# Bias-table reads moved behind four loads, the identity ahead on the SyncE queue, and new landing times in a hand-written plan (T5 attention, then a squared-ReLU FFN)

## The chip, the core and the metric

The kernel runs on one core of a Trainium2 chip. The metric is device time in microseconds (us), the median over several runs. A profile is one execution recorded by the hardware; its times are counted from the first instruction. Engines are named as in the profile: PE (TensorE matmuls), PEld (TensorE weight loads), DVE (VectorE), ACT (ScalarE), POOL (GpSimd, which here only issues DMAs), SP (SyncE, likewise).

## What is computed

Eight batches of attention with eight heads, 576 positions and head size 64, with a bias that depends on the distance of two positions, and then a feed-forward net on all 4608 rows:

```python
scores = scale * np.matmul(q, k.transpose(0, 1, 3, 2))
bias = bias_table[bucket]            # bucket of |i - j|; 31, the last, from 128 on
scores = scores + bias.transpose(2, 0, 1)[None]
attn = exp(scores - max) / (sum + 1e-09)
x = (attn @ v).transpose(0, 2, 1, 3).reshape(4608, 512)
out = np.maximum(x @ w_in, 0.0) ** 2 @ w_out      # 512 -> 2048 -> 512
```

## The kernel before

**Units.** Attention is cut into 96 units: a batch, a block of 192 queries and a pair of heads. A unit's scores are ten PE matmuls (`st`, lines 615 and 640); ACT takes their exponential in two pieces of 960 and 768 columns (`et`, line 666); DVE multiplies the band near the diagonal by exp(bias) from a table `tb_sb` (lines 684 and 698); ten matmuls multiply by V and give the sums as well (`pv`, line 774); ACT makes the reciprocal by a logarithm and an exponential (`r`, lines 816 and 846); DVE multiplies (`x_sb`, line 827). When a block of 192 rows has all four of its head pairs, layer 1 can start on it (`hps`, line 902: eight matmuls to a group, evicted and squared by ACT and DVE in lines 913 to 921), and later layer 2 (`yps`, line 985; eviction in line 998; output by SP in line 1001).

**Loads.** K and Q of the first two batches come in as pairs of heads by POOL's DMAs (`kh`, `qh`, line 251) and are transposed on PE against an identity `id_sb` (line 502; evictions in lines 517 and 519; small copies in line 554). The very first pair of K comes through SP as `raw` and is cast by DVE (line 392). V goes to `vz`, the weights to `w_in_sb` and `w_out_sb`, all by POOL's one queue, in the order in which `load_qk`, `load_v`, `table_read` and `load_w_in` are called (lines 376 to 459). Batches from the third on are transposed by SP's DMAs.

**The bias table.** `bt_sb` and `far_sb` arrive by ACT's queue; DVE subtracts (line 400), ACT exponentiates (line 403), one matmul against a one-hot matrix `oh_sb` spreads the 32 buckets over 512 distances (line 409), DVE casts (line 414), and SP writes the result to memory as `t_bias` (line 418). Three POOL DMAs then read it back as overlapping rows into `tb_sb` (line 421): heads 0 and 1, 2 and 3, and 4 to 7. The first of them waits for SP's write, and POOL issues in order, so what is behind it waits too.

**The order.** Every instruction is an `Op` with an engine, the time that it occupies it, its latency, what it depends on and when it is due. `Plan.run` (line 139) walks through all of them once, at build time, with those numbers, and writes the instructions of each engine in the order that it finds. On the chip each engine runs its list strictly in that order. So a number in the plan takes no time itself, but it sets what stands ahead of what. A load's landing is planned as `dma = max(dma, at + 1.35) + o.load; o.done = dma + 1.9` (lines 175 to 177); before, a pair of Q or K is planned at 1.2 us of the DMA engines, a V load at 1.02 us, and a table read at 0.3 us for each head. `plan.fill` (line 471) puts matmuls that compute nothing needed (`warm`, line 367) wherever PE would be idle in the plan before the first `pv`.

Of the kernel before, what the change touches and what calls it, by code (L numbers as in the profile page):

```python
# [30 lines left out]
PT, TPP = 96, 6  # L31
# [9 lines left out]
F1_LAG, F2_LAG = 4.8, 19.5  # L41

NEXT = 4.0
START = {"POOL": 1.25, "DVE": 0.85, "PE": 1.25, "ACT": 2.9, "SP": 0.3}

MODE = 0.095
WAIT = {"ACT": 0.15, "DVE": 0.05}
# [44 lines left out]
class Plan:  # L92
# [46 lines left out]
    def run(self):  # L139
        free = {**dict.fromkeys(self.streams, 0.0), **START}  # L140
        dma, rows, held = 0.0, 128, None
        while any(q for x in self.streams.values() for q in x.values()):
# [31 lines left out]
            free[eng] = at + o.occ  # L174
            if o.load:
                dma = max(dma, at + 1.35) + o.load
                o.done = dma + 1.9
            if o.instead:
                o.instead()
            self.order.append(o)  # L180
# [4 lines left out]
def kernel(  # L185
# [10 lines left out]
    nc = tc.nc  # L196
# [53 lines left out]
    def dma(eng, out_, in_):  # L250
        return lambda: io(eng.dma_start(out=out_, in_=in_))  # L251
# [4 lines left out]
    def load_qk(b, h0, n, which="kq"):  # L256

        return [
            pool(
                dst[:, h0 : h0 + n, :],  # L260
                src[b, h0 : h0 + n].rearrange("h (p t) d -> p h (t d)", t=TPP),
                0.6 * n,
            )
            for dst, src, name in zip(h16s[b][::-1], (k, q), "kq")
            if name in which
        ][::-1]

    def load_v(b, h, deps=()):

        vz = vzs[b % 2]  # L270
        e, o = h % 2, 64 * (h % 2)
        loads = [
            pool(
                vz[:, 0:4, h, o : o + 64],
                v[b, h, 0:512, :].rearrange("(t p) d -> p t d", p=128),
                1.02,
                deps,
            )
        ]
# [49 lines left out]
    for out_, in_, t in (  # L329
        (bt_sb, bias_table, 3.2),  # L330
        (far_sb, bias_table[NBK - 1 : NBK, :].to_broadcast([NBK, H]), 3.6),
    ):
        dma(nc.scalar, out_, in_)()
        small_in.append(Op("ACT", 0.0, 0.0, None, []))
        small_in[-1].at, small_in[-1].done = 0.0, t
# [22 lines left out]
            )  # L358
        ]

    def small(out_, in_, lat):
        return add("SP", "set", 0.5, lat, dma(nc.sync, out_, in_))
# [52 lines left out]


    loads_qk[0, 4] = loads_qk[0, 5] = load_qk(0, 4, 2)
    written = add("SP", "set", 0.45, 3.5, dma(nc.sync, tdram.ap(), tv_sb), [tv])
    loads_v[0] = [x for h in range(2) for x in load_v(0, h, vz_set[0])]

    def table_read(h0, n):
        return pool(
            tb_sb[:, h0 : h0 + n, :],
            bass.AP(tensor=tdram, offset=512 * h0 + 1, ap=[[1, 128], [512, n], [1, 384]]),
            0.3 * n,
            [written],
        )

    def table_mixed(e):

# [659 lines left out]
```

## Time and profile before

| What | us |
|---|---|
| median of 5 runs | 425.76 (424.82 to 428.29) |
| the profiled execution, as timed | 425.89 |
| its span, first to last instruction | 424.1 |
| PE busy in the span | 407.8 (96%) |
| DVE busy | 315.0 (74%) |
| ACT busy | 302.5 (71%) |
| POOL busy (issuing) | 130.7 (31%) |

The page cuts the span into 40 slices of 10.6 us and gives each engine's busy share in tenths. A window view gives the busy time of each engine in stretches that the reader chooses, with the TensorE clock that was granted there (PEclk, 1.00 is full speed). A timeline lists instructions in order of time, equal neighbours merged, with the idle time before them and what ended it. For a DMA the timeline shows the time in which it is issued; the landing is later, and the view of DMA issues gives the time from the one to the other.

### The profile page before, as it was taken

The page shows a single profiled execution, that of the slowest core. Times are in us where ns is not written, and L with a number is a line of the kernel's source. Part 1 is how long each engine was busy: PE and PEld are TensorE (multiplying, and loading weights), DVE is VectorE, ACT ScalarE, POOL GpSimd, SP SyncE. Part 2 cuts the span into 40 slices and gives each one's busy share as a digit, 9 for nine tenths or more (in the row PEclk, how much of TensorE's full clock was granted, in tenths as well). Part 3 has the DMA queues.
Part 4 walks back from the last instruction along what each step waited for, and adds up shares of the span by engine and source line. Part 5 has one row for each costly group of instructions (what it writes and reads, how often), then busy time and mean ns, then how long its engine had stood idle before and what let it go on. Part 6 is the DMA issues. An engine that isn't in the chain of part 4 may idle for free.

```text
span 424.1 us, 9453 instructions
## 1 busy us (share of the span) xinstructions
PE 407.8 (96%) x3631; PEld 261.9 (62%) x3631; DVE 315.0 (74%) x940; ACT 302.5 (71%) x588; POOL 130.7 (31%) x176
## 2 busy tenths in 40 slices
PE   7979999999899999999999999999999999999996
PEld 4656786566675666666666666665666666565554
DVE  6778866578775777787778787787787877778762
ACT  5899878786797888778877778768877878771000
POOL 6955829606800193006700193006000000000000
PEclk8899999999999999999999999999999999999999
DMA  9999999989982499068974599167203201001012
GB/s 124 157 199 141 152 146 87 111 87 138 125 91 67 73 119 122 28 105 101 105 74 67 104 87 127 38 103 89 38 29 73 64 9 42 22 6 51 25 51 74
DMA packets 164765, 36.61 MB, mean 86 GB/s; under 512 B 152584, under 2 KB 160064, under 8 KB 164720
## 3 DMA queue, kind: packets, MB, share of 16 engines
q0 software_dynamic: 129728, 19.11, 59.5%
q1 hardware_dynamic: 34896, 16.90, 17.3%
q8 instruction: 28, 0.46, 0.5%
q14 instruction: 17, 0.14, 0.1%
q10 hardware_dynamic: 96, 0.00, 0.0%
HBM read 37.56 MB, written 16.52 MB: 128 GB/s over the span
## 4 chain that ended last, share of the span: by engine, by line
PE 78%; DVE 8%; ACT 7%; DMA 4%; issue 2%; SPq 0%; POOLq 0%
PE yps L985 27%; PE hps L902 26%; PE pv L774 13%; PE st L640 6%; ACT et L666 4%; PE pv L748 3%; PE st L615 2%; DMA kt<-k 2%; DVE x_sb L827 2%; ACT r L816 2%; DVE et L684 2%; DMA tb_sb<-t_bias 1%; DVE rt L921 1%; DVE y L998 1%; DVE km_sb L554 1%
## 5 line engine op out<-in xcount | busy, mean ns | idle before, releaser
L666 ACT ACTIVATE et<-st 128x960 f16<-128x960 f32 x192 | 167.9, 882 | 58.9 <-PE st L640 58.1
L902 PE MATMUL hps<-x_sb,w_in_sb 128*128 128x384 f16 (+1 forms) x896 | 150.9, 303 | 1.4 <-DVE rt L921 0.9
L985 PE MATMUL yps<-w_out_sb,g_sb 128*128 128x512 f16 (+1 forms) x592 | 148.5, 373 | 1.8 <-DVE y L998 1.6
L902 PEld LDWEIGHTS <-w_in_sb 128*128 128x128 f16 x896 | 83.0, 98 | 50.8 <-issue 3.6
L684 DVE TENSOR_TENSOR et<-et,tb_sb 128x384 f16<-128x384 f16 (+2 forms) x288 | 78.3, 311 | 35.0 <-ACT et L666 30.4
L251 POOL DMA_DIRECT2D vz<-in_v_dram x80 | 57.9, 744 | 131.6 <-PE pv L774 72.2
L985 PEld LDWEIGHTS <-g_sb 128*128 128x128 f16 x592 | 57.1, 98 | 49.1 <-issue 4.0
L774 PE MATMUL pv<-et,vz 128*128 128x192 f16 x804 | 84.0, 247 | 1.7 <-DVE et L684 1.1
L827 DVE TENSOR_TENSOR x_sb<-pv,r 64x192 f16<-64x192 f32 x192 | 67.8, 353 | 23.2 <-ACT r L846 20.1
L917 DVE TENSOR_TENSOR g_sb<-rt 128x384 f16<-128x384 f16 x192 | 67.5, 355 | 7.9 <-ACT rt L913 4.1
L774 PEld LDWEIGHTS <-vz 128*128 128x128 f16 x804 | 62.0, 98 | 17.2 <-issue 14.6
L816 ACT ACTIVATE r<-pv 64x192 f32<-64x192 f32 x192 | 62.4, 325 | 8.4 <-PE pv L774 3.6
L913 ACT ACTIVATE rt<-hps 128x384 f16<-128x384 f32 x93 | 45.3, 487 | 26.0 <-PE hps L902 25.1
L921 DVE TENSOR_SCALAR rt<-hps 128x384 f16<-128x384 f32 x99 | 55.2, 557 | 11.0 <-PE hps L902 7.3
L640 PE MATMUL st<-qt,kt 64*128 64x192 f16 x768 | 51.0, 246 | 1.6 <-ACT et L666 1.6
L251 POOL DMA_DIRECT2D k<-in_k_dram x48 | 31.0, 682 | 26.0 <-DMA q<-in_q_dram 13.5
L846 ACT ACTIVATE r<-r 128x192 f32<-128x192 f32 x96 | 34.8, 363 | 3.0
L640 PEld LDWEIGHTS <-kt 64*128 64x128 f16 x768 | 31.9, 95 | 4.9 <-issue 3.2
L998 DVE TENSOR_SCALAR y<-yps 128x512 f32<-128x512 f32 (+1 forms) x37 | 25.0, 675 | 7.2 <-PE yps L985 6.5
L615 PEld LDWEIGHTS <-km_sb 128*128 128x128 f16 x192 | 18.3, 98 | 19.0 <-issue 3.8
L615 PE MATMUL st<-qt,km_sb 128*128 128x96 f16 x192 | 24.1, 208 | 1.8 <-ACT et L666 1.1
L251 POOL DMA_DIRECT2D q<-in_q_dram x18 | 24.6, 1401 | 0.0
(33 smaller groups left out, 118.9 us busy)
## 6 DMA issues: line engine op xcount, KB each, us to landing
out_dram<-y SPq DMA_DIRECT2D x35, 256.0 KB, 2.5
vz<-in_v_dram POOLq DMA_DIRECT2D x64, 64.0 KB, 3.4
q<-in_q_dram POOLq DMA_DIRECT2D x18, 192.0 KB, 8.1
k<-in_k_dram POOLq DMA_DIRECT2D x48, 72.0 KB, 7.1
w_in_sb<-in_moe_w_in_dram POOLq DMA_DIRECT2D x4, 512.0 KB, 10.0
w_out_sb<-in_moe_w_out_dram POOLq DMA_DIRECT2D x4, 512.0 KB, 10.0
qh<-in_q_dram POOLq DMA_DIRECT2D x8, 144.0 KB, 6.9
kh<-in_k_dram POOLq DMA_DIRECT2D x7, 144.0 KB, 7.6
```

Of the source, the lines that this page charges most:

```text
L251: return lambda: io(eng.dma_start(out=out_, in_=in_))
L615: nc.tensor.matmul(st[:, g, 2 * IC : 2 * IC + IC // 2], km_sb[:, p % KB, :], qts[p][:, ds(c0 + g * IC // 2, IC // 2)], start=True, stop=True,)
L640: nc.tensor.matmul(st[:, e, ds(i * IC, IC)], kts[p][rows, ts(2 * g + i, 128)], qts[p][rows, ds(c0, IC)], start=True, stop=True,)
L666: io(nc.scalar.activation(out=et, in_=sts[n, g][:, :, 0:w], func=EXPF, scale=SCALE))
L684: nc.vector.tensor_tensor(out=sl, in0=sl, in1=tb_sb[:, 2 * hp : 2 * hp + 2, ds(w0, w)], op=MULT)
L774: nc.tensor.matmul(pv if jt < 4 else pv.rearrange("p (g c) -> p g c", g=2), vz[:, jt, 2 * hp + e, :], ets[n, jt // 2][:, e, ds(jt % 2 * IC ...
L816: nc.scalar.activation(out=rs[n][o : o + 64, :], in_=pvt[n, e][64 - o : 128 - o, 0:IC], func=LNF)
L827: nc.vector.tensor_tensor(out=x_sb[o : o + 64, hp, ds(ring(blk), IC)][:, ::-1], in0=pvt[n, e][o : o + 64, 0:IC], in1=rs[n][o : o + 64, :], ...
L902: nc.tensor.matmul(hps[:, ds(i * w, w)], w_in_sb[:, kk, ts(nt, 128)], x_sb[:, kk, ds(o, w)], start=(kk == 0), stop=(kk == 3),)
L917: io(nc.vector.tensor_tensor(out=g_sb[:, ts(u, k), o : o + w], in0=rt, in1=rt, op=MULT))
L921: io(nc.vector.tensor_scalar_max(out=rt, in0=hpt[blks, u][:, 0 : 2 * IC], scalar1=0.0))
L985: nc.tensor.matmul(ypt[j], g_sb[:, nt, ds(128 * m % RING, 128)], w_out_sb[:, nt, cols], start=(nt == 0), stop=(nt == 15),)
```

## The change

Five edits; the arithmetic is the same.

1. On POOL's queue the V loads of heads 2 and 3 and the K and Q loads of heads 6 and 7 move ahead of the first two table reads, and the V loads of heads 4 and 5 ahead of the third.
2. On SP's queue the identity is issued first, ahead of `raw`.
3. The one-hot matrix `oh_sb` moves from SP's queue to ACT's, as the third DMA there, ahead of the load of ACT's function table.
4. Planned landing times: a Q or K load 0.46 us for each head where it was 0.6, a V load 0.6 and 0.3 where it was 1.02 and 0.5, a table read 0.5 for each head where it was 0.3, 2.0 us after the transfer where it was 1.9, the write of `t_bias` 2.6 us where it was 3.5, `raw` 3.3 where it was 3.4.
5. ACT is planned to be free from 3.3 us on, where it was 2.9.

```diff
-START = {"POOL": 1.25, "DVE": 0.85, "PE": 1.25, "ACT": 2.9, "SP": 0.3}
+START = {"POOL": 1.25, "DVE": 0.85, "PE": 1.25, "ACT": 3.3, "SP": 0.3}
-                o.done = dma + 1.9
+                o.done = dma + 2.0
-                0.6 * n,
+                0.46 * n,
-                1.02,
+                0.6,
-                    0.5,
+                    0.3,
         (far_sb, bias_table[NBK - 1 : NBK, :].to_broadcast([NBK, H]), 3.6),
+        (oh_sb, oh_d.ap(), 4.5),
+    id_in = add("SP", "set", 0.45, 2.8, dma(nc.sync, id_sb, id_d.ap()))
     k_raw = add(
-        "SP", "set", 0.45, 3.4, dma(nc.sync, raw, k[0, 0:2].rearrange("h (p t) d -> p h (t d)", t=TPP))
+        "SP", "set", 0.45, 3.3, dma(nc.sync, raw, k[0, 0:2].rearrange("h (p t) d -> p h (t d)", t=TPP))
     )
-    small_in.append(small(oh_sb, oh_d.ap(), 2.8))
-    id_in = small(id_sb, id_d.ap(), 2.8)
...
-    written = add("SP", "set", 0.45, 3.5, dma(nc.sync, tdram.ap(), tv_sb), [tv])
+    written = add("SP", "set", 0.45, 2.6, dma(nc.sync, tdram.ap(), tv_sb), [tv])
...
-            0.3 * n,
+        return pool(tb_sb[:, h0 : h0 + n, :], rows, 0.5 * n, [written])
...
+    loads_v[0] += [x for h in range(2, 4) for x in load_v(0, h)]
+    loads_qk[0, 6] = loads_qk[0, 7] = load_qk(0, 6, 2)
+    tbs = [table_read(0, 2), table_read(2, 2)]
+    loads_v[0] += [x for h in range(4, 6) for x in load_v(0, h)]
+    tbs += [table_read(4, 4)] * 2
+    loads_v[0] += [x for h in range(6, 8) for x in load_v(0, h)]
...
-    tbs = [table_read(0, 2), table_read(2, 2)]
-    loads_v[0] += [x for h in range(2, 4) for x in load_v(0, h)]
-    loads_qk[0, 6] = loads_qk[0, 7] = load_qk(0, 6, 2)
-    tbs += [table_read(4, 4)] * 2
-    loads_v[0] += [x for h in range(4, 8) for x in load_v(0, h)]
```

Edits 4 and 5 change numbers of the plan alone, and with them the written order on PE, ACT and DVE, all the way to the end of the kernel.

More of the change, by code (lines that the diff above doesn't have):

```diff
@@ L359, in ones @@
         ]
-    def small(out_, in_, lat):
-        return add("SP", "set", 0.5, lat, dma(nc.sync, out_, in_))
     warm = psP.tile([128, 512], FP32, tag="p1", name="warm")
@@ L417 @@
     loads_qk[0, 4] = loads_qk[0, 5] = load_qk(0, 4, 2)
-    written = add("SP", "set", 0.45, 3.5, dma(nc.sync, tdram.ap(), tv_sb), [tv])
+    written = add("SP", "set", 0.45, 2.6, dma(nc.sync, tdram.ap(), tv_sb), [tv])
     loads_v[0] = [x for h in range(2) for x in load_v(0, h, vz_set[0])]
     def table_read(h0, n):
-        return pool(
-            tb_sb[:, h0 : h0 + n, :],
-            bass.AP(tensor=tdram, offset=512 * h0 + 1, ap=[[1, 128], [512, n], [1, 384]]),
-            0.3 * n,
-            [written],
-        )
+        rows = bass.AP(tensor=tdram, offset=512 * h0 + 1, ap=[[1, 128], [512, n], [1, 384]])
+        return pool(tb_sb[:, h0 : h0 + n, :], rows, 0.5 * n, [written])
[5 more added lines that the diff above has]
+    loads_v[0] += [x for h in range(6, 8) for x in load_v(0, h)]
     def table_mixed(e):
```

## The prediction

> **What bounds the kernel now.** I read the page's busy shares first (PE 96%), then windows, to see which stage has room, then the timelines of POOL, DVE and ACT around the table reads, then the landings of the single DMAs. The windows; the columns are length, then busy time and instructions of PE, PEld, DVE, ACT and POOL, the granted PE clock, and the DMA share and rate:
>
> ```profile
> 4.58:8.00 3.42, 2.42 (x45) 1.73 (x47) 2.34 (x9) 2.00 (x6) 2.75 (x5) 1.00 1.25 166
> 8.00:11.41 3.41, 3.10 (x48) 1.99 (x48) 2.20 (x7) 3.26 (x5) 1.43 (x3) 0.50 0.86 61
> 11.41:14.82 3.41, 3.41 (x41) 2.15 (x39) 1.69 (x5) 2.47 (x4) 3.41 (x6) 0.50 1.15 162
> ...
> 15.00:25.00 10.00, 8.28 (x108) 6.41 (x107) 9.61 (x34) 8.66 (x20) 8.27 (x12) 1.00 1.34 183
> 25.00:42.74 17.74, 14.64 (x194) 10.74 (x194) 13.54 (x45) 17.26 (x35) 10.12 (x15) 1.00 1.26 163
> 42.74:60.00 17.26, 16.22 (x216) 14.24 (x215) 13.20 (x42) 13.32 (x29) 10.09 (x12) 1.00 1.42 156
> ...
> 200.00:420.00 220.00, 219.40 (x1765) 134.86 (x1764) 165.84 (x477) 144.99 (x283) 34.14 (x44) 1.00 0.47 61
> ```
>
> From 200 us on PE is busy 219.40 of 220.00: PE is the bound there, and a change can only move the end by letting PE do more useful work early. PE's idle time is in the start: 1.72 of 10.00 us, 3.10 of 17.74, 1.04 of 17.26. In those stages others are the bound: DVE at 9.61 of 10.00 from 15 to 25 us, ACT at 17.26 of 17.74 from 25 to 42.74. Before 15 us the first bias multiply holds everything, as these timelines show, one of POOL, then one of DVE, ACT and PE:
>
> ```profile
> 4.59 2.73 POOL L251 DMA_DIRECT2D vz<-in_v_dram  x4
> 9.98 1.45 POOL L251 DMA_DIRECT2D tb_sb<-t_bias  x2 [2.65 <-DMA t_bias<-tv_sb]
> 11.41 1.53 POOL L251 DMA_DIRECT2D vz<-in_v_dram  x2
> ...
> 17.87 0.83 POOL L251 DMA_DIRECT2D w_in_sb<-in_moe_w_in_dram  x1
> ```
>
> ```profile
> 15.00 2.72 DVE L684 TENSOR_TENSOR et<-et,tb_sb 128x384 f16<-128x384 f16 x12 [1.18 <-DMA tb_sb<-t_bias]
> ...
> 19.89 0.84 DVE L519 CAST kt<-tp 128x288 f16<-128x288 f32 x2
> ...
> 22.22 0.48 DVE L519 CAST qt<-tp 128x288 f16<-128x288 f32 x1
> 22.75 0.26 PE L615 MATMUL st<-qt,km_sb 128*128 128x96 f16 x2 [0.72 <-DVE qt L519]
> 23.33 0.97 ACT L666 ACTIVATE et<-st 128x960 f16<-128x960 f32 x1 [0.54 <-PE st L640]
> 29.19 0.83 PE L902 MATMUL hps<-x_sb,w_in_sb 128*128 128x192 f16 x8
> ```
>
> POOL stands for 2.65 us until SP's write of the table has landed, and all loads behind it are late by as much: V of heads 2 and 3, K and Q of heads 6 and 7, the weights. The fourth head pair is then transposed and evicted in the stage where DVE is the bound (19.89, 22.22), and ACT starves for 0.54 us behind it. The landings of the trace: the last load ahead of the table at 10.33 us, the table reads at 14.98, 15.47 and 19.46, the two V loads at 15.71 and 16.20, K and Q at 16.94 and 17.81, the last V of the batch at 21.26, the four parts of `w_in` at 25.42, 32.09, 37.58 and 40.08.
>
> **Part 1, the first DMAs (identity, raw, one-hot): nothing.** An issue on SP takes 0.45 us. The identity goes from 1.67 to 0.74 and lands, by its 3.40 us, at 4.14 instead of 5.07; `raw` goes from 0.74 to 1.19 and lands, by its 3.35 us, at 4.54 instead of 4.09. The first transposes waited 0.80 us for the identity, until 5.11; now the cast is late: 4.54 and 0.43 give 4.97 for the first half, 0.36 more for the second, which ends the twelve within 0.1 us of before. So one wait takes the other's place. The one-hot matrix, third on ACT at about 1.63, lands at 4.7; its matmul ran at 5.49. ACT's table load moves from 1.66 to 2.1 and ends at 3.4; ACT's first operation was at 4.88. The chain of the table moves by the 0.45 us of `raw`, and one eviction (0.48) comes ahead of its cast on DVE: the write, at 6.64 before, goes out by 7.6 at the latest and lands, after the 2.78 us to 9.42 of before, between 9.5 and 10.4. What hides this is POOL, which now has work until 10.2. Bounds: 0.3 us gained to 0.3 lost.
>
> **Part 2, the loads ahead of the table.** The four loads take POOL 1.53 + 0.68 + 0.69 = 2.9 us, from 7.33 to 10.2. The table's first read is issued at 10.2 instead of 9.98, and everything behind the reads is issued 2.65 us earlier (`w_in` at 15.2 instead of 17.87). The loads ahead of the table in the queue are new: their landings were 0.24, 0.49, 0.74 and 0.87 apart, 2.34 us in all. Where the first read lands is the unknown. At the lowest: Q of the fourth pair at 10.33 + 2.34 = 12.7 by the queue, but not under its 4.28 us from an issue at 9.5, which is 13.8, and 0.49 (the second read's distance to the first) behind it: 14.3. At the highest: the read took 5.00 us on an empty queue, of which the queue shows packets from 11.0 on, 1 us after the issue; 13.8 and 2.3 more for the slowest of the 16 engines give 16.1. I take 15.1, which is the old latency from the new issue (10.2 + 5.0) and in the middle. It is as good as unchanged. The DMA engines' empty time (share 0.00 from 10 to 11 us) goes, so the queue's tail moves: last V of the batch by about 2.4 us, from 21.26 to 18.8, and `w_in` with it, to 23.0, 29.7, 35.2 and 37.7.
>
> The Trainium skill has a rule that speaks against this part. "DMA: Bandwidth & Descriptors", section "Two DMAs through the same engine are not ordered", says that descriptors within one queue of a DMA engine start in order, so the table's read can't pass the four loads; with the fit in its section "Anatomy of one DMA — SWDGE (gpsimd) path", 2.0 us and bytes over 436 GB/s, their 852 KB would be an estimated 1.95 us ahead of it. By that the read's transfer could begin at 12.3, by the rows' 2.34 us at 12.7; the sum is the same by both, since the issue of the last load holds the read until 13.8.
>
> **Part 3, what the earlier loads and the new plan do to the order.** The changed program's order, against the old one: before the first `pv` stand, in addition, the twelve K transposes of the fourth pair, half of its Q's, the scores of a fifth unit and its first exponential, and two of the fourth pair's evictions on DVE; seven `warm` matmuls fewer stand in the last stretch. That takes 0.84 us of evictions out of DVE's 9.61, and 0.48 more goes to ACT: 1.3 us in the stage where DVE is the bound. If the table lands up to about 1 us late, this covers it; ACT, too, has the fifth exponential (0.97) and an eviction (0.42) to do first. On ACT, from 16 us to the end of the twelfth unit's exponentials at 42.74, the work is the same but for one eviction fewer (0.42) and one `rt` more (0.49); the idle 0.19 + 0.18 + 0.54 = 0.9 us there should go. So that point comes **0.8 us** earlier.
>
> At that point the old order has 32 `hps` matmuls done on PE, the new one 56, since its plan has `w_in` landing up to 6 us earlier than the old plan had. 24 more at 0.089 us (88 took 7.81) are 2.1 us; it has three `pv` (0.25) and four `st` (0.27) fewer: **1.6 us** of PE's work ahead. This fits into the 3.10 us that PE was idle from 25 to 42.74. If the loads did not come earlier, the third and fourth parts of `w_in` would hold PE for some 1 us there.
>
> From there on I count nothing: both orders run through a stage in which PE now and then waits for ACT (1.04 us from 42.74 to 60; the new order has its long run of `hps`, 72 matmuls, two units earlier, and three units' exponentials behind it), and from the eighteenth unit on both have the same instructions and the same number of switches between 64 and 128 rows (156). The plan deals them out differently, and single stalls like the 1.11 us at 109.05 may come or go: 1 us to either side.
>
> Sum: 0 + 0.8 + 1.6 = 2.4 us. The profiled execution took 425.89 us, of which 1.8 lie around its span; 423.5 for it, and 423.4 for the median, which lies 0.13 lower: 0.55% faster.
>
> **Rivals.**
> *Hidden anyway.* ACT stays the bound from 16 to 43 us and PE's extra `hps` come out of work that would have fit later; then only the removed starvation, 0.5 to 0.9 us, is left: 425.0. For it: ACT at 97%. Against it: PE idles 5.9 us after 15 us, and needs work in that very time.
> *Slower: the clock.* PE's clock is halved from 8.00 to 14.82 us (its records step at 4.58, 8.00 and 14.82, 3.42 us or twice that apart), and it came back after a window in which PE was busy 3.41 of 3.41, largely with `warm` matmuls; a window with 3.10 of 3.41 did not bring it back. The new order has transposes and scores in place of seven of them, with waits between. If the clock stays at 0.50 to 18.23, the 3.29 us of PE's work there take twice as long; PE's later idle hides about half, so 1.6 to 3.3 us on the forecast, 426 or so. If it stays for the next window too, to 21.65 (another 2.68 us of PE's work), it is 3.0 to 6.0 us: 426.4 to 429.4, and slower than now by what counts if a quarter or less is hidden. It decides from a busy share somewhere between 91% and 100% in the window to 14.82. "TensorE: Matmul & The Clock Gate", section "What's actually happening", gives the window as 3413 ns, which the trace's steps agree with, and says that an idle window throttles; here one with PE busy 71% did (4.58 to 8.00).
> *More than forecast.* If the clock isn't halved at 8.00 at all, since four more `warm` matmuls bridge the gap before 5.1 us, or if PE's idle after the twelfth unit goes too: 2 us more, 421.4.
> *The table is late*, at 16.1: DVE starts 1.1 us later with 1.3 us less to do; the 0.8 us is lost, the 1.6 stays: 424.3.
>
> **How the numbers follow.** What can be told from no change here is about 0.5%, 2.1 us, that is 423.63 to 427.9. Forecast 423.4, with its bounds of 1 us or so to either side: 0.47. Hidden, or the table late: 0.27. The clock for one window more: 0.07; for two, or a row of new stalls of that size: 0.10. More: 0.09. Of the forecast's 0.47 about 0.36 is under 423.63, with all of the last case: faster 0.45. Slower: the 0.10. The rest, 0.45, is the same. The range reaches from the case of more (421.4, and half a us for its own spread) to the upper end of the clock for one window (423.4 + 3.3, and half a us as well): 420.8 to 427.2; the two windows lie beyond it.
>
> **What would show it.** POOL without a wait ahead of the table reads; the first read landing at 14.3 to 16.1; `w_in` issued at about 15.2 and landing by 23; no `kt` eviction of the fourth pair after the first bias multiply; the first `hps` about 1 us earlier than 29.19; PE idle from 25 to 43 us near 2 us; and from 200 us on the same instructions 2 to 3 us earlier. I am wrong if the clock is 0.50 after 14.82, if the table's write lands after 10.4 and POOL waits again, or if PE waits for `w_in`.

## The result, and the profile after

The changed kernel takes **428.0 us** (median of 29 runs, 425.12 to 429.36) against 426.36 (50 runs, 423.82 to 428.54) for the kernel before: a ratio of 1.0037, interval 1.0024 to 1.0050. It is 0.37% slower, where 0.55% faster was forecast. A second series gave 1.0043 (1.0019 to 1.0068). Its first profiled execution took 426.77 us as timed, with a span of 425.0 us (before 424.1). Lines behind the changed part have numbers 4 lower than before (band multiply L680, exponential L662, `pv` L770, `hps` L898, evictions L513 and L515).

The windows of the changed kernel, in the columns of the forecast (PE, PEld, DVE, ACT, POOL busy, granted PE clock, DMA share, GB/s):

```profile
11.41:14.82 3.41, 3.41 (x52) 2.40 (x46) 2.36 (x6) 2.74 (x4) 3.41 (x6) 0.50 0.95 172
15.00:25.00 10.00, 8.13 (x92) 6.12 (x90) 8.02 (x29) 7.77 (x17) 7.12 (x12) 0.78 1.23 173
25.00:42.74 17.74, 15.24 (x210) 12.55 (x204) 15.70 (x52) 16.53 (x34) 11.97 (x17) 1.00 1.35 162
42.74:60.00 17.26, 15.13 (x207) 12.33 (x202) 12.65 (x41) 14.16 (x28) 8.65 (x11) 1.00 1.55 162
...
200.00:420.00 220.00, 219.70 (x1767) 134.73 (x1764) 163.76 (x474) 145.26 (x283) 33.20 (x43) 1.00 0.46 61
```

From 15 to 25 us DVE has fallen from 9.61 to 8.02 and ACT from 8.66 to 7.77: both wait, and the clock there was 0.78, not 1.00. From 25 to 42.74 PE does more (15.24, before 14.64), from 42.74 to 60 less (15.13, before 16.22). From 200 us on PE is busy all the time, as before. Three timelines, of POOL, of DVE and of PE, show the table and what stood ahead of it:

```profile
9.55 0.69 POOL L251 DMA_DIRECT2D qh<-in_q_dram  x1
10.85 1.45 POOL L251 DMA_DIRECT2D tb_sb<-t_bias  x2 [0.62 <-DMA t_bias<-tv_sb]
...
15.99 0.81 POOL L251 DMA_DIRECT2D w_in_sb<-in_moe_w_in_dram  x1
```

```profile
15.48 0.48 DVE L515 CAST kt<-tp 128x288 f16<-128x288 f32 x1 [0.91 <-PE tp L498]
16.29 0.48 DVE L515 CAST kt<-tp 128x288 f16<-128x288 f32 x1 [0.33 <-PE tp L498]
16.80 2.71 DVE L680 TENSOR_TENSOR et<-et,tb_sb 128x384 f16<-128x384 f16 x12
20.41 0.74 DVE L823 TENSOR_TENSOR x_sb<-pv,r 64x192 f16<-64x192 f32 x2 [0.90 <-ACT r L842]
```

```profile
15.80 0.45 PE L498 MATMUL tp<-id_sb,kh 96*64 96x96 f16 x6
16.18 0.40 PE L365 MATMUL warm<-km_sb 128*128 128x128 f16 x2
16.37 0.37 PE L611 MATMUL st<-qt,km_sb 128*128 128x96 f16 x2
...
17.92 1.30 PE L770 MATMUL pv<-et,vz 128*128 128x192 f16 x7
```

POOL's wait for the table's write shrank from 2.65 to 0.62 us. The first table read landed at 15.23, as forecast (15.1), and `w_in` from 23.89 on (23.0). So the transfers did what they should. But when the table was there, DVE did not use it: in its list two evictions of the fourth pair stand first, and they waited 0.91 and 0.33 us for PE, which worked its longer list at half clock. The first bias multiply came at 16.80 (before 15.00), the first `pv` at 17.92 (15.41), the first `x_sb` at 20.41 (17.63). The last two in the kernel before:

```profile
15.41 2.00 PE L774 MATMUL pv<-et,vz 128*128 128x192 f16 x20
```

```profile
17.63 0.73 DVE L827 TENSOR_TENSOR x_sb<-pv,r 64x192 f16<-64x192 f32 x2
```

### The profile page after: what moved, and what is told of

It is laid out like the page before. It is cut to its first block, busy times and chain, and to the rows that moved or that the text cites. A ratio compares the mean times of both kernels' runs of the same rounds, so it can differ in the third digit from the quotient of the medians.

```text
span 425.0 us, 9452 instructions
## 1 busy us (share of the span) xinstructions
PE 408.2 (96%) x3628; PEld 263.3 (62%) x3628; DVE 313.5 (74%) x940; ACT 302.2 (71%) x588; POOL 130.9 (31%) x176
## 4 chain that ended last, share of the span: by engine, by line
PE 80%; DVE 9%; ACT 5%; DMA 3%; issue 2%; SPq 0%; DVEq 0%
PE yps L981 27%; PE hps L898 26%; PE pv L770 14%; PE st L636 7%; PE pv L744 3%; ACT et L662 2%; DVE x_sb L823 2%; PE st L611 2%; DVE rt L917 2%; DMA kt<-k 2%; ACT r L812 2%; DVE et L680 1%; DVE y L994 1%; DVE g_sb L913 1%; ACT r L842 1%
## 5 line engine op out<-in xcount | busy, mean ns | idle before, releaser
L662 ACT ACTIVATE et<-st 128x960 f16<-128x960 f32 x192 | 167.6, 882 | 54.1 <-PE st L636 53.4
L898 PE MATMUL hps<-x_sb,w_in_sb 128*128 128x384 f16 (+1 forms) x896 | 151.8, 303 | 2.7 <-DVE qt L515 1.2
L898 PEld LDWEIGHTS <-w_in_sb 128*128 128x128 f16 x896 | 83.5, 98 | 52.8 <-issue 4.2
L680 DVE TENSOR_TENSOR et<-et,tb_sb 128x384 f16<-128x384 f16 (+2 forms) x288 | 77.9, 311 | 33.2 <-ACT et L662 29.9
L770 PE MATMUL pv<-et,vz 128*128 128x192 f16 x804 | 85.8, 248 | 3.9 <-DVE x_sb L823 1.6
L770 PEld LDWEIGHTS <-vz 128*128 128x128 f16 x804 | 63.2, 98 | 20.1 <-issue 16.7
L909 ACT ACTIVATE rt<-hps 128x384 f16<-128x384 f32 x98 | 47.7, 487 | 31.6 <-PE hps L898 31.4
L917 DVE TENSOR_SCALAR rt<-hps 128x384 f16<-128x384 f32 x94 | 52.4, 558 | 10.8 <-PE hps L898 7.0
## 6 DMA issues: line engine op xcount, KB each, us to landing
w_out_sb<-in_moe_w_out_dram POOLq DMA_DIRECT2D x4, 512.0 KB, 10.3
```

The costliest lines, as they stand in the source:

```text
L662: io(nc.scalar.activation(out=et, in_=sts[n, g][:, :, 0:w], func=EXPF, scale=SCALE))
L680: nc.vector.tensor_tensor(out=sl, in0=sl, in1=tb_sb[:, 2 * hp : 2 * hp + 2, ds(w0, w)], op=MULT)
L770: nc.tensor.matmul(pv if jt < 4 else pv.rearrange("p (g c) -> p g c", g=2), vz[:, jt, 2 * hp + e, :], ets[n, jt // 2][:, e, ds(jt % 2 * IC ...
L898: nc.tensor.matmul(hps[:, ds(i * w, w)], w_in_sb[:, kk, ts(nt, 128)], x_sb[:, kk, ds(o, w)], start=(kk == 0), stop=(kk == 3),)
L917: io(nc.vector.tensor_scalar_max(out=rt, in0=hpt[blks, u][:, 0 : 2 * IC], scalar1=0.0))
```

## Where the time lies: two measures

**PE's useful work.** I add up the columns of all matmuls but the fill at the rate that the traces show at full clock, and read in each trace when so much of it was done. The starts of equal matmuls lie 82 ns apart for 192 columns and 216 for 512; two that use half of the array's rows or columns start within 4 ns of each other, so each of these counts half. That makes 366.4 us of work in every kernel. The table is worked out that way; its entries are us against the first profile of before, positive is later. A number behind a name marks a further profile of the same kernel; the other names are explained below.

| work done (time in before) | before_2 | after | after_2 | after_3 | f_dma | b_loads | h_ba26 | h_pool |
|---|---|---|---|---|---|---|---|---|
| 2 us (10.5) | +1.6 | +0.7 | +0.8 | +1.7 | +0.9 | +1.5 | +0.5 | +1.1 |
| 6 us (18.6) | +1.1 | +2.3 | +1.1 | +3.4 | +1.4 | +1.3 | +0.2 | +1.6 |
| 12 us (30.9) | +0.70 | +0.71 | -0.50 | +3.14 | +0.94 | +0.89 | -0.70 | +0.73 |
| 25 us (50.4) | +0.68 | -1.41 | -2.62 | +1.02 | +0.89 | -0.35 | -2.09 | -0.67 |
| 60 us (90.9) | +0.66 | +1.85 | +0.63 | +4.26 | +0.89 | +2.06 | +2.15 | +3.56 |
| 150 us (190.2) | -0.47 | +1.78 | +0.21 | +4.11 | +1.08 | +1.55 | +5.60 | +1.64 |
| 350 us (404.1) | -0.69 | +0.87 | -0.54 | +3.11 | +1.01 | +1.33 | +5.97 | +1.33 |

Two things can be read off it. The executions of the changed kernel differ from each other almost only ahead of 31 us (from there on the distances of `after`, `after_2` and `after_3` change by less than 0.4 us). Those of before differ once more: between 91 and 190 us `before_2` gains 1.1 us on the first profile, in which PE waited 1.11 us at 109.05. And between 31 and 91 us these three executions of the changed kernel lose the same: 1.14, 1.13, 1.12 us.

**The clock.** PE starts at half clock in every trace: the first matmuls, of 512 columns, start 427 ns apart, where 216 is full rate. In 13 of the 20 profiles of this case it then has full clock for one window of 3.41 us, from about 5 us on, falls back, and has the half-clock windows counted here. Each of them takes 0.004 off the mean granted clock of a 424 us span, so the mean counts them: 0.992 is two, 0.988 three, 0.984 four, 0.980 five. In the other seven profiles (a mean of 0.994 or more) the clock's records begin only with a return to full clock, between 15.8 and 23.0 us; the views print 1.00 ahead of it, but PE was at half clock from the start. `before_2`, with its first record at 16.42 us, took 0.82 us for the eight matmuls that took 0.50 in the first profile of before, whose records have full clock there:

```profile
7.49 0.50 PE L640 MATMUL st<-qt,kt 64*128 64x192 f16 x8
```

```profile
8.89 0.82 PE L640 MATMUL st<-qt,kt 64*128 64x192 f16 x8
```

How long an execution of that kind ran at half clock, its mean doesn't tell. All executions whose mean clock is known:

| half-clock windows behind the first full one | before: executions, median us | after: executions, median us |
|---|---|---|
| two | 20, 425.00 | 5, 425.99 |
| three | 21, 425.80 | 4, 426.80 |
| four or five | none | 17, 428.52 |
| half clock from the start (mean 0.994 or more) | 68, 426.22 | 18, 427.88 |

With as many windows the changed kernel is about 1.0 us slower (0.99 and 1.00), about the loss of the rows from 31 to 91 us. The rest, as far as it can be counted, is that 17 of its 26 executions have four windows or more, and none of 41 before. In the last row it is 1.65 us slower, and what part of that is clock is not shown. Here are the windows of its second profile (two) and of its third (five):

```profile
11.50:14.90 3.40, 3.40 (x50) 2.39 (x46) 2.39 (x6) 2.73 (x4) 3.40 (x6) 0.50 1.04 184
14.90:18.30 3.40, 3.32 (x51) 2.19 (x48) 2.85 (x11) 3.14 (x5) 3.40 (x6) 1.00 1.39 181
18.30:21.80 3.50, 2.20 (x26) 1.77 (x25) 3.28 (x13) 3.28 (x10) 2.58 (x4) 1.00 1.23 185
```

```profile
11.50:14.90 3.40, 3.40 (x54) 2.25 (x50) 2.32 (x7) 2.86 (x5) 3.40 (x5) 0.50 1.03 174
14.90:18.30 3.40, 3.40 (x40) 1.97 (x40) 2.13 (x6) 2.55 (x5) 3.40 (x6) 0.50 1.28 172
18.30:21.80 3.50, 3.50 (x29) 2.94 (x26) 2.54 (x12) 2.55 (x6) 2.78 (x5) 0.50 1.24 171
21.80:25.20 3.40, 1.57 (x21) 1.38 (x20) 2.93 (x12) 2.81 (x8) 1.26 (x2) 1.00 1.29 201
25.20:28.60 3.40, 3.40 (x27) 2.81 (x26) 2.24 (x7) 1.87 (x4) 2.32 (x3) 0.50 1.27 204
```

Up to 14.9 us PE is busy in both (3.40 of 3.40, at 0.50), and then one gets the clock and the other does not. Where it stays at 0.50, PE is the bound in a stage in which ACT and DVE should be: ACT falls to 2.55 of 3.40, from 3.14.

Busy time does not sort these windows: in the first profile of before, 2.42 busy of 3.42 us (4.58 to 8.00) was followed by half clock, and 2.20 of 3.50 in `after_2` was not. How much of the array was at work does. For each matmul I take the rows and columns of the array that it uses, as a share of 128 x 128 (`hps`, most `pv` and the fill 1, `st` against `kt` 0.5, a transpose 0.375), times the time that its columns take at the clock of the moment, as a share of the window; by the steps above that is 0.42 ns a column at full clock, and 0.83 at half, where 96 columns take 80 ns. In all 20 traces, up to 415 us:

| windows at | share of the array at work | followed by |
|---|---|---|
| half clock | up to 0.738 (52 windows) | half clock |
| half clock | 0.745 and more (42) | full clock |
| full clock | up to 0.36 (21) | half clock |
| full clock | 0.363 to 0.382 (4) | three times full, once half clock |
| full clock | 0.39 and more (2296) | full clock |

The half-clock windows of `before` have 0.58 and 0.75, those of `after_2` 0.65 and 0.76, those of `after_3` 0.70, 0.71, 0.67 and 0.95. The third of these (14.97 to 18.38) holds transposes, scores and fill but no `pv`; in `f_dma`, with the lists of before, the window from 14.3 to 17.7 has `pv` in it and 0.87. And `after_3`'s full window from 21.8 us has 0.35, hence its fifth. Where the windows fall differs between executions, and so does what is in them. The weights were chosen with the traces at hand, and no run was made to test them.

## The experiments

### What the moved transfers and the new lists do, each by itself

`f_dma`: the lists of before (planned with its numbers), GpSimd's transfers in the changed order. `f_first`: the same for the first DMAs alone. `f_order`: the changed kernel's lists, transfers in the old order. `a_late4`: the changed kernel, with the fourth pair's transposes planned behind the first table read. Of the edits, that of `f_dma` at the end of the build (`ahead` moves loads in front of a table read) and that of `a_late4`:

```diff
-    for o in plan.run():
+    order = plan.run()                       # f_dma, on the kernel before
...
+    ahead([*loads_v[0][4:6], loads_qk[0, 6][1], loads_qk[0, 6][0]], tb0)
+    ahead(loads_v[0][6:8], tb2)
+    for o in order:
```

```diff
-   [loads_qk[b, 2 * hp][w] or casts[u], id_in, *(kq_ready[0] if p == 1 else [])],
+   [loads_qk[b, 2 * hp][w] or casts[u], id_in, *(kq_ready[0] if p == 1 else []), *(tbs[:1] if p == 3 else [])],
```

> The kernel before with every engine's list as it was, and only POOL's queue in the changed order (four loads ahead of the first two table reads, two ahead of the third). Theory A, the loss lies in the lists that the new plan numbers wrote: this is as fast as before or up to 0.3% faster, the first bias multiply within 0.5 us of 15.0 us, the weights 2 to 2.7 us earlier and little made of it, because the old lists ask for them late. Rival B, the loss lies in the table reads standing behind the loads: 0.3 to 0.5% slower than before, the first bias multiply at 16 us or later with DVE waiting for the table.

> The changed kernel with all its lists on PE, ACT, DVE and SP as they are, and only POOL's queue put back into the old order. Theory A: 0.3 to 0.7% slower than before, the fourth pair's K evictions on DVE ahead of the first bias multiply, which starts at 17 us or later since K of that pair lands at about 17 now. Rival B: within 0.15% of before.

> The kernel before with every compute list as it was, and only the first DMAs changed: identity, then raw on SP, the one-hot matrix third on ACT. Rival C, raw's 0.45 us is what is lost: the first scores 0.4 to 0.5 us later than 7.31 and 0.1 to 0.15% slower than before. Theory A: the first scores at most 0.2 us later, since the identity gates the first transposes before and raw gates them now, and no difference that can be told.

> The changed kernel, with one dependency more in the plan alone: the transposes of the fourth pair of K and Q may not be planned before the first table read has landed, so that their evictions stand behind the first bias multiplies in DVE's list. The rest of the lists is planned anew. Theory A: the first bias multiply at 15.2 to 15.6 us instead of 16.80, and 0.2 to 0.6% faster than the changed kernel, so between 0.2% faster and 0.2% slower than before. Rival D, a third window of half clock is the loss, whatever the lists: still 0.3 to 0.4% slower than before, with the clock at 0.50 until 18 us or later.

Measured: `f_dma` 426.31, ratio 1.0010 (0.9998 to 1.0023); `f_first` 425.81, 0.9992 (0.9978 to 1.0007); `f_order` 430.53, 1.0104 (1.0086 to 1.0122); `a_late4` 434.72, 1.0209 (1.0193 to 1.0225). With the old lists the earlier transfers bring nothing, though `w_in` landed at 23.32 in place of 25.42: the first `pv` came at 16.66, behind scores, exponentials and fill at half clock, and from 31 us on the column of `f_dma` in the table stays between +0.9 and +1.1. So neither the reads behind the loads nor the first DMAs cost anything that can be told from nothing, and the loss lies in the lists. `f_order` agrees: these lists without the early loads wait for K and lose 1.0% (I had expected 0.3 to 0.7%). `a_late4` did not undo the loss: its first bias multiply came at 15.44, but the first `pv` only at 17.47, since PE's list still had the fifth unit's scores ahead; and it met a new stall at 118 us, of which more below.

### Which of the plan's numbers

The plan of the changed kernel has the first table read at 15.69 us, that of before at 14.14; the chip had it at 15.23 and 14.98. `b_tbl` plans it 1.55 us later in the kernel before, `a_tbe` 1.55 us earlier in the changed one. `b_loads` gives the kernel before the new costs of the K, Q and V loads, and nothing else: its lists are those of before up to 20 us, and nearly the changed kernel's from there on. `h_ba26` takes the changed kernel, with the lists of before up to 26 us of the plan. `p_half` lets its planner take PE's instructions twice as long from 8 to 17 us. None of them moves the first loads; later transfers stand where the new plan puts them.

```diff
                 o.done = dma + 1.9
+                if o in self.table:           # b_tbl; the first two table reads
+                    o.done += 1.55
```

```diff
-                0.6 * n,                      # b_loads
+                0.46 * n,
-                1.02,
+                0.6,
-                    0.5,
+                    0.3,
```

```diff
+            slow = 0.0                    # p_half
             if eng == "PE":
...
+                slow = o.occ if HALF[0] < at < HALF[1] else 0.0
-            o.at, o.done = at, at + o.lat
-            free[eng] = at + o.occ
+            o.at, o.done = at, at + o.lat + slow
+            free[eng] = at + o.occ + slow
```

> The kernel before with one number of its plan changed: the first two table reads are planned to land 1.55 us later (15.69 instead of 14.14, which is where the changed kernel's plan has them). No DMA moves. In its lists the fifth unit's scores and both its exponentials now stand ahead of the first pv and the first ln (before: four units), the 4th pair's transposes stay behind the pv as before. Theory P (the loss comes from where the plan places the table, because the planner fills the time up to it with work that the strict lists then put ahead of the first pv): first pv about 2 us later than the 15.41 of before, first x_sb at 19.5 to 20.5 instead of 17.63, and a time 1.0 to 2.5 us over before (ratio 1.0025 to 1.006). Theory Q (the loss of the changed kernel is in its late lists, or in the 4th pair's transposes and evictions alone): first pv later, but the time within 0.8 us of before, since ACT only does exponentials early that it would do later.

> The changed kernel with one number of its plan changed: the first two table reads are planned to land 1.55 us earlier (14.14 instead of 15.69). No DMA moves. In its lists four units' scores stand ahead of the first pv as in before, with six of the 4th pair's transposes, and no eviction of the 4th pair ahead of the first bias multiply. Theory P: first bias multiply at 15.2 to 15.6 (changed kernel 16.80), first pv at 16.4 to 17 (17.92), first x_sb at 18.5 to 19.2 (20.41), time 1.2 to 2.5 us under the changed kernel's 428.0, so 425.5 to 426.8, a ratio to before of 0.9985 to 1.002. Theory Q (late lists): within 0.8 us of the changed kernel, ratio 1.002 to 1.006.

> The changed kernel with the three engines' lists of before up to 26 us of plan time (by script), and from there on planned with the changed kernel's numbers; DMAs as in the changed kernel. If the loss lies in the early lists (theory P): the first 26 us as with the kernel before's lists under the new DMA order (first pv 16.5 to 16.9, first x_sb 18.9 to 19.2), and a time of 425.3 to 426.8 (ratio 0.998 to 1.001). If it lies in the late lists (theory Q): as the changed kernel, 427.4 to 428.6 (ratio 1.0025 to 1.006). If the plan made for other numbers is worth about a microsecond by chance alone, anything from 425 to 428, and then the equal-work table shows the difference arising behind 30 us.

> The changed kernel with a planner that takes TensorE instructions at twice their time between 8 and 17 us of plan time, as the records show the clock at 0.50 there; all else and every DMA unchanged. Its lists have three units' scores ahead of the first pv (changed kernel five, before four), one fill matmul pair instead of four groups, and the 4th pair's transposes behind the first pv. Theory P (a plan that is wrong about the early stage puts the wrong work first): first bias multiply at the table's landing (15.2 to 15.5), first pv by 15.9, first x_sb at 17.8 to 18.3, and the early transfers now gain: a time of 424.0 to 425.6, ratio to before 0.995 to 0.999. If instead ACT's total work up to the twelfth unit sets the pace whatever is first (theory S: the order within the early stage is worth nothing, ACT is busy all along): 425.8 to 428.5.

> The kernel before with only the plan's costs of the K, Q and V loads set to those of the changed kernel (0.46 for 0.6 per head of K or Q, 0.6 for 1.02 and 0.3 for 0.5 per V load); no DMA moves, and the table keeps its planned landing (14.06 against 14.14). Up to the second ln its lists are those of before; from about 20 us on they are nearly the changed kernel's (VectorE's list matches the changed kernel's in 94% of its instructions, that of before in 64%). Theory P (the loss comes from the table's planned landing, in the first 25 us): no loss, within 0.8 us of before, ratio 0.998 to 1.002. Theory L (the late lists that the new load costs write lose by themselves: feed-forward work taken early and paid back, key transposes issued among the next batch's copies): 1.5 to 4 us over before, ratio 1.0035 to 1.010, with the difference arising between 45 and 65 us or at 115 to 123 us.

> The changed kernel once more, unchanged, for a second profile and for its ratio on the same chip as the others: 1.002 to 1.006. If the start (end of the first unit's exponentials, 10.28 in its first profile, 9.54 in the kernel before's) is set by where the clock's windows fall in that run, it moves by up to a microsecond between two profiles of one kernel; if it is set by the changed first DMAs it stays at 10.2 to 10.4.

> The kernel before once more, unchanged, for a second profile. If the start is set by where the clock's windows fall in a run: end of the first unit's exponentials anywhere from 9.5 to 10.8 (9.54 in its first profile; 10.76 in a kernel whose lists and DMAs are the same up to there). If the first profile is typical, 9.4 to 9.7.

Measured: `b_tbl` 427.98, ratio 1.0063 (1.0039 to 1.0086); `a_tbe` 430.83, 1.0128 (1.0108 to 1.0149); `h_ba26` 432.32, 1.0170 (1.0143 to 1.0197); `p_half` 433.06, 1.0178 (1.0158 to 1.0199); `b_loads` 426.83, 1.0017 (0.9998 to 1.0037); `after_2` 427.81, 1.0043 (1.0019 to 1.0068); `before_2` has one time, 425.21. The first unit's exponentials end at 11.10 in `before_2` (9.54 in the first profile) and at 10.36 in `after_2` (10.28; in two later profiles 11.25 and 10.53): the start differs by over a microsecond between executions of one kernel, and the changed first DMAs can't be seen in it.

`b_tbl` says that the table's planned landing alone makes the kernel 0.6% slower: with it a fifth unit's scores and both its exponentials stand ahead of the first `pv` (17.92), and of its four countable executions two have four or more half-clock windows. The three repairs failed, all by more than the loss that they should repair, though their early part went about as expected (first bias multiply at 15.32, 15.16 and 15.32). In the table `h_ba26` is 0.70 us ahead of before at 31 us, loses 2.9 by 91 and 3.5 more by 190. So there are two further places behind 26 us.

**The first is from 31 to 91 us.** `b_loads` has the early part of before and nearly the late lists of the changed kernel, and it loses about the same there, 1.17 us (0.89 to 2.06), while `f_dma` and `before_2`, with the lists of before, lose nothing (0.94 to 0.89, 0.70 to 0.66). Its ratio as a whole, 1.0017, can't be told from 1. The sums of the windows from 31 to 67 us, of before, of after and of `b_loads`, show idle PE:

```profile
sum 36.00, PE 33.33 PEld 27.12 DVE 28.06 ACT 30.70 POOL 20.46; mean PE 5.55 PEld 4.52 DVE 4.68 ACT 5.12 POOL 3.41
```

```profile
sum 36.00, PE 32.18 PEld 26.87 DVE 29.70 ACT 30.50 POOL 22.09; mean PE 5.36 PEld 4.48 DVE 4.95 ACT 5.08 POOL 3.68
```

```profile
sum 36.00, PE 32.83 PEld 26.75 DVE 29.35 ACT 30.80 POOL 20.90; mean PE 5.47 PEld 4.46 DVE 4.89 ACT 5.13 POOL 3.48
```

PE is busy 33.33, 32.18 and 32.83 us. At the end of the twelfth unit's exponentials the changed kernel has 56 `hps` done and before 32, as forecast; but then three units of attention stand behind the long run of `hps`, and PE has only their short steps to do. Its waits from 31 to 91 us (the lines of 0.2 us and more) add up to 2.8 us in before, 4.7 in after and 4.1 in `b_loads`; those for DVE's `x_sb` grow from 0.8 to 1.7 and 1.8. That the lead is lost by this order of work is my reading; shown is that the late lists lose it. The lead of 1.41 us at 50 us has become a lag of 1.85 at 91.

**The second is near 118 us**, and the changed kernel itself is spared: DVE waits for the keys of the pair numbered 12 (from 0), which SP transposes. `h_pool` and `a_pool` test what holds them.

### The stall at 118 us

In `h_ba26` the two transposes are issued at 110.53 and 112.97, among eleven transfers by which POOL copies the next batch's queries and keys. They take 9.2 and 7.8 us; in before, where they are issued at 117.9 and 119.5, behind the last of those transfers, they take 4.1 and 3.0. In before:

```profile
qt<-q SPq DMA_TRANSPOSE x1, 4.1
kt<-k SPq DMA_TRANSPOSE x1, 3.0
```

DVE's wait for them in `h_ba26`, from 100 to 132 us (us in total, times, longest):

```profile
DVE km_sb L576 <- DMA kt<-k: 3.8, 1, 3.8
```

The edit lets POOL read one element of the transposed keys before it issues the copies:

```diff
+    mark = Op("POOL", 0.0, 0.0, lambda: io(nc.gpsimd.tensor_copy(out=mark_sb, in_=kts[p][0:1, 0:1])), [])
+    i = order.index(behind) + 1              # behind: the transpose of the 12th pair's keys
+    order[i:i] = [mark, *held]               # held: the copies, taken from where they stood
```

> The changed kernel with the lists of before up to 26 us (432.3 us, a ratio of 1.017) and one more edit: GpSimd reads one element of the 12th pair's transposed keys before it issues the copies of the fourth batch's queries and keys to DRAM, so that these eleven transfers start when the transposes have landed instead of beside them. If the transposes' long flight among these transfers (9.2 and 7.8 us, against 4.1 and 3.0 in before, where they are issued behind the transfers) is what stalls VectorE for 3.8 and TensorE for 3.4 us at 116 to 121 us: flight 3 to 5 us, the stall under 1 us, no half-clock window at 124 us, and a time 3 to 5 us lower, 427 to 429.3. If the transposes are late because of SyncE's own queue (the output write in front of them, which waits 11 us for its data): the flight shortens but the stall stays over 2 us, and the time stays at 430 to 433.

> The changed kernel with its own lists, except that GpSimd reads one element of the 12th pair's transposed keys before it issues the copies of the fourth batch's queries and keys, so that these start when the transposes have landed. If executions of the changed kernel lose time there in part of its runs (theory T): flight of the two transposes 3 to 5 us instead of 8.2 and 7.3, median 0.8 to 2 us under the changed kernel's 427.8 to 428.0, ratio to before 0.999 to 1.002. If the loss is in the first 25 us alone (theory P): within 0.6 us of the changed kernel, ratio 1.003 to 1.006.

> The changed kernel, a third profile. Theory T: the two transposes at 108 and 110 us land between 116 and 121 us, and where they land past 118 VectorE waits for them and the end is later by as much. Theory P: they land by 117.5 as before, and the whole spread between profiles lies in the first 20 us (end of the fifth unit's exponentials at 21.0 or 22.2 by two or three half-clock windows).

> As after_3, a fourth profile of the changed kernel, read in the same way.

Measured: `h_pool` 427.26, ratio 1.0026 (1.0000 to 1.0052), where `h_ba26` had 1.0170. The two transposes, in the DMA views of `h_ba26` and of `h_pool` (the last number is us from issue to landing):

```profile
qt<-q SPq DMA_TRANSPOSE x1, 9.2
kt<-k SPq DMA_TRANSPOSE x1, 7.8
```

```profile
qt<-q SPq DMA_TRANSPOSE x1, 2.7
kt<-k SPq DMA_TRANSPOSE x1, 2.7
```

The wait on them is gone, though an output write stands in front of them on SP as before. So it was the transfers beside them. That is what held `h_ba26` back; in `a_late4`, `a_tbe` and `p_half`, where it was not tested, DVE waits for transposed keys as well, 4.9, 2.7 and 5.3 us at the longest. It does not explain the changed kernel: `a_pool` took 427.81, 1.0047 (1.0027 to 1.0068), no gain, although its transposes, too, went from 8.2 and 7.3 to 2.7 and 2.8. `after_3` (429.0) and `after_4` (429.03) have no stall there either; they have five half-clock windows, in `after_3` from 8.1 to 21.8 and from 25.2 to 28.6 us. What I had expected of these runs to show a loss at 118 us is refuted, and the early clock takes its place.

### Does the fill set the number of windows?

`b_nofill` and `a_nofill` leave the plan's fill out of PE's list (24 matmuls in before, 21 in after), `a_fill2` makes each twice as long. Nothing else in the lists changes.

```diff
+    fill = plan.fill[2]
     for o in plan.run():
-        o.fn()
+        if o.fn is not fill:
+            o.fn()
```

> The kernel before without the plan's fill (the 24 or so 128x128 matmuls on zeros that stand in TensorE's list ahead of the first transposes, scores and pv up to the first pv; the six 128x512 ones at the start stay). The lists are else the same, and no result depends on them. Theory C (the half-clock windows follow TensorE's activity): more half-clock windows than before's two or three, 4 or 5 in most executions, and 1 to 3 us longer, ratio 1.002 to 1.007. If the windows come by themselves: the same number, and the time within 0.5 us or up to 0.6 us shorter, since the six fills that stand ahead of the first pv go.

> The changed kernel without the plan's fill (27 matmuls), else the same lists. Theory C: half-clock windows in even more executions, 4 to 6, and 0.5 to 2.5 us over the changed kernel, ratio to before 1.005 to 1.010. If the windows come by themselves: 427.3 to 428.2, ratio 1.002 to 1.006.

> The changed kernel with every fill matmul twice as long (128x256 in place of 128x128), else the same lists. Theory C: fewer half-clock windows, two or three in most executions, and a time of 426 to 427.4, ratio 1.000 to 1.003, less what the longer fill delays (up to 0.1 us for each of the two ahead of the fifth unit's scores). If the windows come by themselves: 427.8 to 428.8, ratio 1.004 to 1.007.

Measured: `b_nofill` 425.77, ratio 0.9995 (0.9978 to 1.0012); `a_nofill` 426.44, 1.0016 (1.0000 to 1.0032); `a_fill2` 425.98, 1.0003 (0.9975 to 1.0030; its runs spread from 424.54 to 430.44). The fill is worth nothing in before. In the changed kernel both edits, in opposite directions, took away, by their medians, more than half of the loss, but their intervals overlap with that of the changed kernel (1.0024 to 1.0050), so this is not shown. Counted by windows, more fill goes with fewer of them: in `a_fill2` three countable executions have two and two have three, in `a_nofill` one has three and two have more, in `b_nofill` none has two, five have three and one has four. The times do not follow, and few can be counted: seven of the twelve executions of `a_fill2` were at half clock from the start, its slowest (430.44) until 17.3 us and once more from 24.1 to 27.5.

No version beats the kernel before: `f_first` at 0.9992 and `b_nofill` at 0.9995 can't be told from it.

## Why the prediction was wrong, step by step

- **What bounds the kernel**: right for the end (PE) and as a list of bounds for the stages. But all of it was read from one execution with two half-clock windows, and 20 of 109 executions of before are of that kind. The start alone varies: the first unit's exponentials end at 9.54 in that profile, at 11.10, 10.76 and 11.03 in three others with the same instructions up to there (`before_2`, `b_tbl`, `b_loads`), all three at half clock from the start.
- **Part 1, the first DMAs, nothing**: right (`f_first`). The write of the table went out at 7.25, within the 7.6 at the latest; it landed not by 10.4, but at about 10.8, since POOL's wait for it ended at 10.85. I had named that as a sign of being wrong; it cost POOL 0.62 us and `w_in` 0.8 (issued at 15.99, not 15.2), and the end nothing that `f_first` shows.
- **Part 2, the transfers**: right. The table at 15.23 (15.1), `w_in` at 23.89, 29.38, 34.92 and 37.44 (23.0, 29.7, 35.2 and 37.7). By themselves, with the old lists, they are worth nothing that can be told (`f_dma`).
- **Part 3, "that point comes 0.8 us earlier": this step failed.** The end of the twelfth unit's exponentials came at 45.01, 43.78, 47.43 and 46.89 in four profiles, before at 42.74 and 43.67: later, in each of the four, than in either profile of before. I took 1.3 us of evictions out of DVE's stage and let the table's lateness be covered by them. What I did not price was when PE reaches the work that was moved ahead: at half clock the fourth pair's transposes and the fifth unit's scores were done at 17.9 us, and DVE and ACT, bound to their lists, waited for them with the table at hand. That work also loads less of the array than the fill and the `pv` in whose place it stood, and the clock stayed at half for longer. The plan's numbers for the transfers came nearer to the chip, but it plans PE at full clock. Whether that mismatch alone is the cause is not shown: `p_half` put the early work right (first bias multiply at 15.32), but lost elsewhere.
- **Part 3, "1.6 us of PE's work ahead"**: the lead was there (56 `hps` against 32; 1.41 us at 50 us). **"From there on I count nothing" failed**: the lead was not kept. The stretch from 31 to 91 us costs 1.1 us in every profile of the changed kernel, and `b_loads` shows that the late lists alone do it. I named the stage's pattern (a long run of `hps`, three units' exponentials behind it), and should have charged the lead to it: work done early by PE counts only if PE has something left to do when the others fall behind.
- **The rival "the clock"** has the right mechanism, transposes and scores in place of fill, but not its price: in the changed kernel one window more costs 0.8 us and two or three more 2.5 (425.99, 426.80, 428.52), where I had 1.6 to 3.3 and 3.0 to 6.0. That these medians lie near the absolute times that I gave (426 or so, and 426.4 to 429.4) is luck, since those start from the forecast's 423.4, which no execution of the changed kernel reached. I gave it 0.17; three windows or more came in 21 of its 26 countable executions, and also in 21 of 41 before. My point of decision, a busy share between 91% and 100%, is refuted: 3.40 of 3.40 kept 0.50 twice in `after_3`. What sorts the windows in the table above is the share of the array at work, with the step at 0.74. "TensorE: Matmul & The Clock Gate", section "What's actually happening", says that one busy window releases the clock, and that the windows run freely, so that the number at the start varies between runs. The second is what the profiles show (two, three and five in one program); the first holds here only if busy means that share, not the busy time of the profile.
- **The rivals "hidden anyway", "the table late" and "more"**: the table was not late. Hidden anyway is nearest to what `f_dma` shows, for the transfers alone.

Shown, then: the transfers are worth nothing that can be told; the new lists cost about 1.0 us between 31 and 91 us; the rest, some 0.6 to 0.9 us of the median, goes, where it can be counted, with more half-clock windows ahead of 29 us, to which the early lists lead (17 of 26 executions with four or more, against none of 41; two of four in `b_tbl`). Which window keeps the clock at 0.50 follows in all 20 traces from the share of the array at work in it. **Open**: how much the executions at half clock from the start lose by the clock, whether a run made to lift that share would win the windows back, and whether the early work placed behind the first `pv`, with nothing else planned anew, would.

## What to carry to other kernels

Where a planner writes strict lists, a better number for one transfer changes all that is planned behind it: price the new lists, not the number, and first ask at which time each engine really reaches what now stands ahead of the critical wait. Work that the bound engine does early is a gain only if it isn't starved later; follow the lead to the place where both orders have done the same. And in a stage under a varying clock, look at several executions and count the half-clock windows, those ahead of the clock's first record too, before reading a difference of 1 us out of two profiles. A busy PE is no sign that the clock will come: look at how much of the array its matmuls use.

## What the runs showed of the hardware that I had not expected

- One program gets two to five half-clock windows of 3.41 us behind its first full one, at about 1 us each (medians of the changed kernel 425.99, 426.80, and 428.52 for four or five), or runs at half clock from the start until 15.8 us or later; the profile's granted clock reads 1.00 in that stretch.
- The array's work in a window, rows times columns times columns streamed, sorts 94 half-clock windows without an exception at 0.74, and 2321 full-clock ones, but for four, near 0.37. PE's busy time doesn't: 2.42 of 3.42 us at full clock was followed by half clock, 2.20 of 3.50 was not.
- A transpose by SP's DMA took 2.7 us alone and 7 to 10 us beside POOL's copies of queries and keys to memory (2.7 in `h_pool`, 6.9 in `after_4`, 10.3 in `a_tbe`).
